# Sliding-window attention with a gated feed-forward on one core: one batch of products with v per unit, w2 measured by groups, and another prologue

## The chip, the core and the metric

The kernel runs on one core of a Trainium2 chip. The core has TensorE (PE; its weight loads are shown apart as PEld), VectorE (DVE), ScalarE (ACT), GpSimd (POOL) and SyncE (SP), which issues most DMAs. Each engine takes its instructions in a fixed order and waits on semaphores for the others. The metric is device time in microseconds (us) of one execution; lower is better.

## The reference

Input is one sequence of 2048 tokens with 512 channels. It is normalised per token; from the result come causal attention with a window of 256 (32 heads of 16 channels) and a gated feed-forward with 1792 hidden channels, and both are joined:

```python
def _A_ref(x, wqkv, wo):
    H = 32; Dh = D // H; W = 256
    q, k, v = ...(x @ wqkv)...
    scores = einsum("bhqd,bhkd->bhqk", q, k) * Dh ** -0.5
    mask = (idx[:, None] - idx[None, :] >= 0) & (idx[:, None] - idx[None, :] < W)
    p = softmax(where(mask, scores, -1e9))
    return (p @ v).reshape(B, S, D) @ wo

def _B_ref(x, w1, w3, w2):
    return (silu(x @ w1) * (x @ w3)) @ w2

xn = layernorm(x)
out = x + _A_ref(xn, A_wqkv, A_wo) * silu(_B_ref(xn, B_w1, B_w3, B_w2))
```

All is float32. The kernel makes most products from 16-bit halves: each operand is split into a high and a low float16 part, and three of the four partial products are summed. Before that every weight is scaled by a power of two that follows from the sums of squares of its columns.

## The kernel before

**Work.** The tokens are cut into four tiles of 512 (`t`), the heads into four groups of eight (`g`), and each group into two halves (`p`). One (`t`, `g`, `p`) is a unit; there are 32. A unit's attention has two passes. The first, `pass1`, makes scores with the queries on the rows of the array (L588), and VectorE takes their maxima (L600). The maxima go through a small transpose (L615), a copy `mt` (L621) and two DMAs into extra rows of `qa`, so that the second pass subtracts them inside its matmuls. `pass2` makes the scores again, with the keys on the rows (L662), in five chunks (four for the first tile); VectorE adds masks (L669), ScalarE takes the exponential into a buffer `pt` (L672), and `values` multiplies `pt` by v in float32 on array tiles of 64 x 32 (L690). `finish` then copies the sums out of the bank `po` into `os`: ScalarE one half (L700), VectorE adds the other (L703).

**Banks.** PSUM has two buffers `s` of two banks for scores, one buffer `po` of two banks, and two banks `m0`, `m1` for the dense products. `po` takes the products with v, and in between the scores of a few parts of the first pass.

**Order on TensorE.** TensorE's order is that of the code; the other engines' order comes from a scheduler. A plan, `PLAN` (`FIRST_PLAN` for the first tile), cuts a unit into five batches. In it W is one chunk of the second pass of this unit, M a part of the first pass of the unit after the next one, in a buffer `s`, X such a part in `po`; the numbers are the chunks whose products with v follow. Between the batches `spread` puts dense work: projections (L534), v (L504), w1 and w3 (`gate_up`, L836), w2 (`down`, L881), wo (`total`, L923). A batch with products counts 2.5 per chunk when the dense work is dealt out, a dense matmul counts 1. Small pieces can be queued some steps on (`later`), or to the next part of a first pass, whose bank then has room beside the scores (`beside_scores`, `maxima`, `besides`).

**Weights.** In the first tile of tokens, w1, w3 and w2 come from memory in 14 blocks `f` of 128 hidden channels, are measured, scaled and split, used, and stored in `dW1`, `dW2` for the other tiles. `load` fetches all three of a block; `measure` takes two blocks: six squares (`squares`, L231 on ScalarE, L233 on VectorE), their sums over partitions by matmuls with ones and the powers of two (`powers`, L258 or L263, L269 to L278), then the cuts of w1 and w3 (`split_pool`: L303 and L304 on ScalarE, L300 on GpSimd). `measure_down` finds one scale for each of the four groups of w2 and queues its cuts. All such tiles lie in 41 slots of 2 KB a partition, taken in turn.

**Prologue.** Token tiles 0 and 2 are fetched by SyncE's queue, 1 and 3 by ScalarE's. VectorE takes means and variances (L406, L407), a reciprocal root by a shifted integer and three Newton steps (`rstd`, L411 to L421), and centres the tokens (L424). TensorE transposes them (L440), ScalarE copies the high halves XH (L443). Meanwhile the weights of q and k of the first group are measured and cut (L290 to L295), and TensorE is kept busy with products of ones (`keep_busy`, L1108). The first projection (L534) needs all four XH and the cut weights.

## Time and profile before

| | us |
|---|---|
| median of 3 runs | 861.09 (858.77 to 861.37) |
| the profiled execution, time | 861.01 |
| its span in the profile | 859.2 |
| TensorE busy in the span | 820.9 |
| granted TensorE clock, mean | 0.992 |

The profile is of one execution. The page gives busy times, the chain of work that ended last, and groups of instructions by line; the trace behind it answers for timelines, waits and stretches of time. A matmul's end is modelled, since matmuls overlap, so distances between starts are the better measure. In a row of a timeline stand the start, the length from first start to last end, engine, line, operation, what is written and read, and in brackets the idle time before and what ended it.

### The profile page before, as it was taken

Reading aid. Unit: us, or ns where it says so; the run is one execution under the profiler, and the core shown is the slowest. Engines: PE = TensorE matmul, PEld = TensorE weight load, DVE = VectorE, ACT = ScalarE, POOL = GpSimd, SP = SyncE. Lnnn points to the kernel's source line nnn. Section 1 sums busy time; section 2 is a strip of 40 time slices with the busy share of each in tenths; the row PEclk is TensorE's granted clock in tenths of the full one; section 3 lists DMA queues with packets and bytes.
Section 4 is the critical chain, followed back from the end, with each engine's and each line's share of the span. In section 5 each row is a group of like instructions: output and inputs, shape, how many; then the busy total and the mean of one; then the engine's idle time right before and its main releaser. Section 6 shows DMA issues by size and latency. Waiting matters only on the chain.

```text
span 859.2 us, 22511 instructions
## 1 busy us (share of the span) xinstructions
PE 820.9 (96%) x8734; PEld 380.0 (44%) x8734; DVE 608.3 (71%) x2013; ACT 407.9 (47%) x598; POOL 198.0 (23%) x325
## 2 busy tenths in 40 slices
PE   9899888899999999998999999999999999999998
PEld 4344334444444444443444444444444444444444
DVE  8786656976787667797777876677676787675435
ACT  6898776273426444344343445443443444433521
POOL 2254256151113203111111112120211113031211
PEclk9999899999999999999999999999999999999999
DMA  9958446236643443452533432534442353333201
GB/s 303 292 195 258 144 143 183 74 101 193 174 121 89 116 118 110 147 151 64 132 104 86 144 104 80 164 118 106 143 128 89 102 153 84 112 102 90 62 13 59
DMA packets 95323, 110.62 MB, mean 129 GB/s; under 512 B 17200, under 2 KB 60528, under 8 KB 95216
## 3 DMA queue, kind: packets, MB, share of 16 engines
q1 hardware_dynamic: 94928, 108.67, 43.5%
q8 instruction: 68, 1.11, 0.6%
q10 hardware_dynamic: 288, 0.52, 0.2%
q14 instruction: 39, 0.32, 0.1%
HBM read 76.28 MB, written 28.57 MB: 122 GB/s over the span
## 4 chain that ended last, share of the span: by engine, by line
PE 57%; DVE 15%; issue 7%; DMA 7%; ACT 7%; POOL 4%; SPq 3%; DVEq 0%; POOLq 0%; ACTq 0%
PE m L836 20%; PE m L881 12%; PE po L690 6%; PE m L534 6%; DVE junk L600 5%; PE m L923 3%; POOL slot L300 3%; PE s L662 3%; PE m L504 3%; DVE s L669 2%; PE s L588 2%; ACT pt L672 1%; DMA slot<-in_A_x_dram 1%; DMA dr<-dd 1%; SPq L734 1%
## 5 line engine op out<-in xcount | busy, mean ns | idle before, releaser
L300 POOL TENSOR_TENSOR slot<-slot,slot 128x256 f16<-128x256 f32 (+1 forms) x228 | 149.5, 681 | 568.1 <-ACT slot L860 446.2
L836 PE MATMUL m<-XH,slot 128*128 128x512 f16 x896 | 267.5, 380 | 2.7 <-DVE slot L851 1.9
L672 ACT ACTIVATE pt<-s,es 128x1024 f32<-128x1024 f32 x152 | 167.8, 1113 | 198.9 <-DVE s L669 186.4
L836 PEld LDWEIGHTS <-slot 128*128 128x128 f16 x1344 | 125.1, 98 | 158.5 <-issue 16.3
L836 PE MATMUL m<-XL,slot 128*128 128x512 f16 x448 | 169.8, 379 | 0.0
L881 PE MATMUL m<-slot,slot 128*128 128x512 f16 x672 | 159.5, 387 | 3.1 <-DVE slot L851 1.9
L600 DVE CUSTOM_DVE_ANT_0 junk<-s,MW 128x320 bf16<-128x320 f32 x288 | 139.6, 485 | 30.8 <-PE s L588 20.1
L669 DVE TENSOR_TENSOR s<-s,MK 128x256 f32<-128x256 f32 (+2 forms) x280 | 118.8, 434 | 55.3 <-PE s L662 51.1
L881 PEld LDWEIGHTS <-slot 128*128 128x128 f16 x672 | 63.1, 99 | 84.0 <-issue 14.4
L690 PE MATMUL po<-pt,V 64*32 64x320 f32 (+4 forms) x2880 | 84.8, 345 | 1.3 <-ACT pt L672 1.1
L600 DVE CUSTOM_DVE_ANT_0 junk<-po,MW 128x320 bf16<-128x320 f32 x160 | 77.3, 483 | 6.7 <-DVE M L600 0.5
L860 ACT CAST slot<-slot 128x512 f16<-128x512 f32 x56 | 34.6, 618 | 74.9 <-DVE slot L856 72.8
L851 DVE SCALAR_TENSOR_TENSOR slot<-slot,m 128x512 f32<-128x512 f32 x56 | 38.4, 685 | 32.1 <-ACT slot L847 32.0
L690 PEld LDWEIGHTS po<-pt,V 64*32 64x32 f32 x2880 | 47.1, 106 | 30.8 <-issue 5.5
L662 PE MATMUL s<-qa,KA 50*64 50x320 f16 (+3 forms) x1472 | 58.0, 259 | 1.7 <-ACT pt L672 0.9
L847 ACT ACTIVATE slot<-m,sgs 128x512 f32<-128x512 f32 x56 | 38.3, 683 | 41.8 <-PE m L836 39.7
L662 PEld LDWEIGHTS <-KA 50*64 50x64 f16 x1472 | 32.6, 105 | 56.4 <-issue 36.1
L588 PE MATMUL s<-KA,qa 48*64 48x320 f16 (+2 forms) x648 | 46.5, 299 | 6.5 <-DVE M L600 3.6
L856 DVE SCALAR_TENSOR_TENSOR slot<-m,slot 128x512 f32<-128x512 f32 x56 | 38.4, 686 | 17.9 <-PE m L836 17.3
L897 DVE SCALAR_TENSOR_TENSOR slot<-m,dsc,slot 128x512 f32<-128x512 f32 x48 | 35.7, 745 | 20.0 <-PE m L881 19.9
L588 PEld LDWEIGHTS <-qa 48*64 48x64 f16 x1024 | 29.6, 106 | 39.8 <-issue 26.6
L534 PE MATMUL m<-XH,whi 128*128 128x512 f16 x120 | 45.5, 387 | 1.6 <-DVE slot L897 0.9
(151 smaller groups left out, 880.7 us busy)
## 6 DMA issues: line engine op xcount, KB each, us to landing
slot<-dW SPq DMA_DIRECT2D x126, 256.0 KB
slot<-in_B_w_dram SPq DMA_DIRECT2D x42, 256.0 KB
dW<-slot SPq DMA_DIRECT2D x42, 256.0 KB
slot<-in_A_x_dram SPq DMA_DIRECT2D x30, 256.0 KB
KA<-dK SPq DMA_DIRECT2D x24, 288.0 KB
qa<-dQ SPq DMA_DIRECT2D x32, 192.0 KB
dK<-slot SPq DMA_DIRECT2D x16, 256.0 KB
dQ<-slot SPq DMA_DIRECT2D x16, 256.0 KB
```

The source lines that it names most:

```text
L300: op(out[:, c], a[:, c], b[:, c])
L534: nc.tensor.matmul(cell["pp"], a[:, k, c, :], b[:, c, :], start=(c, i) == parts[0][0], stop=(c, i) == parts[-1][-1])
L588: nc.tensor.matmul(s[64 * c:64 * c + 64, r, :n], qa[rows, 2 * p + a, ii * P + 64 * c:ii * P + 64 * c + 64], ka[rows, 2 * p + a, e - n:e], ...
L600: nc.vector.tensor_tensor_reduce(out=junk[:, :n], in0=s[:, r, :n], in1=mask, scale=1.0, scalar=NEG, op0=ALU.add, op1=ALU.max, accum_out=M[ ...
L662: nc.tensor.matmul(s[64 * h:64 * h + 64, r, o:o + 64 * n], ka[rows, 2 * p + a, 64 * (m + 4):64 * (m + 5)], qa[rows, 2 * p + a, 64 * (m + k ...
L669: nc.vector.tensor_add(v, v, MK[:, kind, of:of + n, :].unsqueeze(1).to_broadcast([P, 2 * len(which), n, 64]))
L672: nc.scalar.activation(pt, s, AF.Exp, scale=es)
L690: nc.tensor.matmul(cell["po"][32 * i:32 * i + 32, h, 64 * (m + k):64 * (m + k + n)], V[64 * h:64 * h + 64, (4 * t + m // 2) % VB, hd * VW: ...
L836: nc.tensor.matmul(cell[k], w[:, (a * NC + c) * P:(a * NC + c + 1) * P], b[:, c, :], start=c == 0 and i == 0, stop=c == NC - 1 and i == 2)
L851: nc.vector.scalar_tensor_tensor(sg, sg, 1.0, cell[0], op0=ALU.add, op1=ALU.mult)
L856: nc.vector.scalar_tensor_tensor(sg, cell[1], 0.5 * HS / (WS * XS)**2, sg, op0=ALU.mult, op1=ALU.mult)
L881: nc.tensor.matmul(ps, hh[:, a * TW + b * P:a * TW + (b + 1) * P], w[:, c * D:(c + 1) * D], start=f == f0 and i == 0, stop=f == f1 - 1 and ...
```

## The change

It has four parts.

1. `values` is called once a unit, with all chunks, in the last batch. The X parts move from batches 1 to 3 into batches 2 to 4, the two chunks WW into batch 4. `pt` has five buffers (`ppool`), not four, and the slots go from 41 to 39.
2. w2 leaves `load` and `measure`. `load_down` fetches its blocks one by one, `measure_down` squares one block at a time on ScalarE, and at a group's last block takes the group's sums by `powers` beside scores, then the scale, then queues the cuts. `measure` has four squares.
3. The scale of a weight is no longer a reciprocal and a product but one integer operation on the power of two's bits. The root takes a step of higher order and one Newton step, with the constants folded in.
4. Token tile 0 is fetched in two halves by two queues, tile 1 by SyncE, 2 and 3 by ScalarE; the scale is ordered ahead of the centring; there are 25 and 3 fillers for 27 and 5.

```diff
-SLOTS = 41
+SLOTS = 39
...
-    ppool = pool("ppool", 4)
+    ppool = pool("ppool", 5)
...
# powers
+            if inv is not None:
+                lasts["scale"] = nc.vector.tensor_scalar(inv.bitcast(I32), al.bitcast(I32), -1.0,
+                                                         (2 * 127 - 63 + WS_EXP) * 2.0**23, op0=ALU.mult, op1=ALU.add)
             nc.vector.tensor_scalar(p2, al, 2.0**63, None, op0=ALU.mult)
-            nc.vector.reciprocal(inv, p2)
...
# prepare: load, rstd
+            if t == b == 0:
+                for h in range(2):
+                    r = slice(64 * h, 64 * h + 64)
+                    (nc.scalar if h else nc.sync).dma_start(xts[b][r], x[r, :])
+                return
+            (nc.scalar if t == 0 and b > 1 else nc.sync).dma_start(xts[b], x[t * TW + b * P:t * TW + (b + 1) * P, :])
...
-            for i in range(3):
+            nc.vector.tensor_mul(sq, r0, r0)
+            nc.vector.tensor_mul(sq, sq, ve)
+            nc.vector.scalar_tensor_tensor(sq, sq, -10 / 3, sq, op0=ALU.add, op1=ALU.mult)
+            nc.vector.scalar_tensor_tensor(r0, sq, 5.0, r0, op0=ALU.add, op1=ALU.mult)
+            with nullcontext() if t else tc.issue_after(lasts["cast"].ins):
                 nc.vector.tensor_mul(sq, r0, r0)
-                nc.vector.scalar_tensor_tensor(sq, sq, -0.5, ve, op0=ALU.mult, op1=ALU.mult)
-                nc.vector.scalar_tensor_tensor(r0, sq, 1.5, r0, op0=ALU.add, op1=ALU.mult)
-            nc.vector.tensor_scalar(rs[:, b0:b1], r0, XS, None, op0=ALU.mult)
+            nc.vector.scalar_tensor_tensor(sq, sq, -0.5 * (3 / 8)**3 * XS, ve, op0=ALU.mult, op1=ALU.mult)
+            nc.vector.scalar_tensor_tensor(rs[:, b0:b1], sq, 1.5 * (3 / 8) * XS, r0, op0=ALU.add, op1=ALU.mult)
...
# load, measure, measure_down
-        nc.sync.dma_start(raw2, w2[f * P:(f + 1) * P, :])
...
-        sb = squares([raws[0][0], raws[1][0], raws[0][1], raws[1][1], RAW[f][1], RAW[f + 1][1]], on_act=6 if f > 2 else 4, apart=apart)
+        sb = squares([raws[0][0], raws[1][0], raws[0][1], raws[1][1]], on_act=4 if f > 2 else 2, apart=apart)
...
+    def load_down(f):
+        RAW2[f] = raw = take(F32)
+        nc.sync.dma_start(raw, w2[f * P:(f + 1) * P, :])
+
+    def measure_down(k, f):
+        f0, f1 = GROUPS[k]
+        n = f1 - f0
...
+        nc.scalar.activation(sq, RAW2[f], AF.Square, accum_out=NORMS[k][:, f - f0:f - f0 + 1])
+        if f < f1 - 1:
+            return
+        sb = small.tile([P, n], BF16, name="sb2")
+        nc.vector.tensor_copy(sb, NORMS[k])
+        def scale(s):
+            p2 = small.tile([P, n], F32, name="pp2")
+            return then(s, powers(sb, n, p2, None, s), lambda: rest(p2))
...
+        beside_scores(2, scale)
...
# plans
-    FIRST_PLAN = (("WMX", ()), ("WMX", ()), ("WMX", ()), ("WM", (0, 1)), ("M", (2, 3)))
-    PLAN = (("WMX", ()), ("WMX", ()), ("WWX", ()), ("WM", (0, 1, 2)), ("MM", (3, 4)))
+    FIRST_PLAN = (("WM", ()), ("WMX", ()), ("WMX", ()), ("WMX", ()), ("M", (0, 1, 2, 3)))
+    PLAN = (("WM", ()), ("WMX", ()), ("WMX", ()), ("WWX", ()), ("MM", (0, 1, 2, 3, 4)))
...
# prologue
-    keep_busy(27)
+    keep_busy(25)
...
-    keep_busy(5)
+    keep_busy(3)
     rstd0(0, 4)
-    for b in range(4):
-        centre0(b)
-    with tc.issue_after(lasts["centre"].ins):
-        qk[0][3]((1,))
+    with tc.issue_after(lasts["scale"].ins):
+        for b in range(4):
+            centre0(b)
+    qk[0][3]((1,))
```

On TensorE, in a unit of a later tile of tokens, the two groups of products with v stood apart before, the first ahead of a product for v (L504), the second, after 12 dense matmuls and eight score matmuls, ahead of one with wo (L923). Rows of equal matmuls are put together with their count; `po`, `pt` and `V` are the sums, the exponentials and v.

```order
L690 MATMUL po<-pt,V 32x256 x8
L690 MATMUL po<-pt,V 32x320 x8
L690 MATMUL po<-pt,V 32x192 x8
L504 LDWEIGHTS XH
L504 MATMUL m_5900<-wvh,XH 128x512
```

```order
L690 MATMUL po<-pt,V 32x320 x8
L690 MATMUL po<-pt,V 32x128 x4
L690 MATMUL po<-pt,V 32x64 x8
L690 MATMUL po<-pt,V 32x128 x4
L923 LDWEIGHTS slot_2418
L923 MATMUL m_5976<-slot_4177,slot_2418 128x512
```

The changed program, same unit, has one group (its line is now 698), behind the eight score matmuls of the last batch.

```order
L698 MATMUL po<-pt,V 32x256 x8
L698 MATMUL po<-pt,V 32x320 x8
L698 MATMUL po<-pt,V 32x192 x8
L698 MATMUL po<-pt,V 32x320 x8
L698 MATMUL po<-pt,V 32x128 x4
L698 MATMUL po<-pt,V 32x64 x8
L698 MATMUL po<-pt,V 32x128 x4
L950 LDWEIGHTS slot_3945
```

The matmuls are the same; the first 24 moved behind the dense work and the scores that stood between. Six dense matmuls follow the group now, where 12 followed each of the two, and between WWX and the last batch stand 18.

On VectorE, at the change from one unit to the next, the addition into `os` was followed before, within the first batch, by the maxima of an X in the other use of `po` (`junk<-po`) and by the copy `mt` from it.

```order
L703 TENSOR_TENSOR os_6333<-os_6333,po_6226 128x512
L669 TENSOR_TENSOR s_6361<-s_6361,MK_119 128x4x2x64
L851 SCALAR_TENSOR_TENSOR slot21_6357<-slot21_6357,m0_6344 128x512
L600 ISA junk_6378,M_6360<-s_6373,MW_111 128x320
L600 ISA M_6360 128x1
L600 ISA junk_6380,M_6360<-s_6373,MW_111 128x320
L600 ISA M_6360 128x1
L600 ISA junk_6389,M_6360<-po_6382,MW_111 128x320
L600 ISA M_6360 128x1
L600 ISA junk_6391,M_6360<-po_6382,MW_111 128x320
L600 ISA M_6360 128x1
L621 CAST mt_6393<-po_6382 32x128
```

In the changed program (lines 711, 677, 878, 608 and 883 do what 703, 669, 851, 600 and 856 did) the next rows from `po` come a batch later.

```order
L711 TENSOR_TENSOR os_6354<-os_6354,po_6305 128x512
L677 TENSOR_TENSOR s_6375<-s_6375,MK_119 128x4x2x64
L878 SCALAR_TENSOR_TENSOR slot9_6371<-slot9_6371,m0_6278 128x512
L608 ISA junk_6392,M_6374<-s_6387,MW_111 128x320
L608 ISA M_6374 128x1
L608 ISA junk_6394,M_6374<-s_6387,MW_111 128x320
L608 ISA M_6374 128x1
L883 SCALAR_TENSOR_TENSOR slot9_6371<-m1_6397,slot9_6371 128x512
L677 TENSOR_TENSOR s_6423<-s_6423,MK_119 128x4x64
```

The X, its maxima and `mt` moved behind the next dense products; 24 dense matmuls stand on TensorE between the last product with v and the next X, where 12 stood, with few exceptions.

In the prologue, VectorE before: the end of the root, the four centrings (L424), and between them the steps of the scale `sw` of the first weights.

```order
L421 TENSOR_SCALAR rs<-r_303 128x4
L424 TENSOR_SCALAR slot_163<-slot_163,mv,rs 128x512
L269 TENSOR_SCALAR al<-s 128x1
L424 TENSOR_SCALAR slot_165<-slot_165,mv,rs 128x512
L275 TENSOR_SCALAR al<-al 128x1
L424 TENSOR_SCALAR slot_167<-slot_167,mv,rs 128x512
L277 TENSOR_SCALAR p2qk_283<-al 128x1
L424 TENSOR_SCALAR slot_169<-slot_169,mv,rs 128x512
L278 RECIPROCAL invqk_284<-p2qk_283 128x1
L384 TENSOR_SCALAR es_355<-p2qk_283 128x1
L290 TENSOR_SCALAR sw_293<-invqk_284 128x1
```

The same place in the changed program:

```order
L270 TENSOR_SCALAR al<-s 128x1
L429 SCALAR_TENSOR_TENSOR rs<-sq,r_289 128x4
L276 TENSOR_SCALAR al<-al 128x1
L280 TENSOR_SCALAR sw_274<-al 128x1
L282 TENSOR_SCALAR p2qk_273<-al 128x1
L432 TENSOR_SCALAR slot_162<-slot_162,mv,rs 128x512
L432 TENSOR_SCALAR slot_165<-slot_165,mv,rs 128x512
L432 TENSOR_SCALAR slot_167<-slot_167,mv,rs 128x512
L432 TENSOR_SCALAR slot_169<-slot_169,mv,rs 128x512
```

The scale is done ahead of the centring. On ScalarE the first cut of the weights (`whi`) accordingly moved from between the second and third copy of XH to ahead of the first.

More of the change, by code (lines that the diff above doesn't have):

```diff
@@ L40 @@
 XS = 2.0**10
-WS = 2.0**13
+WS_EXP = 13
+WS = 2.0**WS_EXP
 QS = 2.0**5
@@ L242, in cast @@
         def cast():
-            nc.vector.tensor_copy(sb, ssq)
+            lasts["cast"] = nc.vector.tensor_copy(sb, ssq)
         if apart:
@@ L324, in scale @@
             p2 = const.tile([P, 1], F32, name=f"p2{name}")
-            inv = const.tile([P, 1], F32, name=f"inv{name}")
-            def rest():
-                cell["p2"], cell["inv"], cell["sw"] = p2, inv, scaled(inv, WS, f"sw{name}")
-            return then(s, powers(cell["sb"], 1, p2, inv, s), rest)
+            cell["p2"], cell["sw"] = p2, const.tile([P, 1], F32, name=f"sw{name}")
+            return then(s, powers(cell["sb"], 1, p2, cell["sw"], s))
         def cut(apart=0):
@@ L364, in scale @@
             p2 = const.tile([P, 1], F32, name=f"p2qk{g}")
-            inv = const.tile([P, 1], F32, name=f"invqk{g}")
-            def rest():
-                cell["p2"], cell["sw"] = p2, scaled(inv, WS, f"sw{g}")
-            return then(s, powers(cell["sb"], 1, p2, inv, s), rest)
+            cell["p2"], cell["sw"] = p2, const.tile([P, 1], F32, name=f"sw{g}")
+            return then(s, powers(cell["sb"], 1, p2, cell["sw"], s))
         def cut(ks=(1, 0)):
@@ L761, in load @@
             return
-        RAW[f] = raw, raw2 = [take(F32) for _ in range(2)], take(F32)
+        RAW[f] = raw = [take(F32) for _ in range(2)]
         for k, w in enumerate((w1, w3)):
@@ L765, in load @@
                               w[:, f * P:(f + 1) * P].rearrange("(c p) f -> p c f", p=P))
[L766 removed]
     measured = set()
     def measure(f, apart=0):
[L772 to L773 removed]
+        raws = [RAW.pop(f + i) for i in range(2)]
+        sb = squares([raws[0][0], raws[1][0], raws[0][1], raws[1][1]], on_act=4 if f > 2 else 2, apart=apart)
         def scale(s=None):
[L776 to L778 removed]
+            pp = small.tile([P, 2, 2], F32, name="pp")
+            pi = small.tile([P, 2, 2], F32, name="pi")
+            return then(s, powers(sb, 4, pp.rearrange("p a b -> p (a b)"), pi.rearrange("p a b -> p (a b)"), s),
                         lambda: rest(pp, pi))
@@ L965, in feed_forward @@
                 if t == 0:
-                    if f % 2 or f == 0:
-                        pieces += [(0, lambda f=f: load(0, f)) for f in (range(f + LEAD, min(f + LEAD + 2, FB)) if f else range(4, LEAD + 1))]
+                    if (f % 2 or f == 0) and f + LEAD < FB - 2:
+                        pieces += [(0, lambda f=f: load(0, f)) for f in (range(f + LEAD, f + LEAD + 2) if f else range(4, LEAD + 1))]
+                    elif f + LEAD == FB - 1:
+                        pieces += [(0, lambda f=f: load(0, f)) for f in range(FB - 2, FB)]
                     if f % 2 and f + 3 < FB:
                         pieces.append((0, lambda f=f + 3: measure(f, 1)))
-                    pieces += [(0, lambda k=k: measure_down(k)) for k, (_, f1) in enumerate(GROUPS) if f == f1 - 1]
+                    pieces += [(0, lambda f=f: load_down(f)) for f in range(f + 2 if f else 0, min(f + 3, FB))]
+                    for m in range(f + 1 if f else 0, min(f + 2, FB)):
+                        k = next(k for k, (_, f1) in enumerate(GROUPS) if m < f1)
+                        pieces.append((0, lambda k=k, m=m: later(2, lambda: measure_down(k, m))))
                 else:
```

54 lines of the change are left out of this document (26 added, 28 removed).

## The prediction, made before the changed kernel was run

> **What bounds the kernel now.** I began with the page: busy shares and the chain of work that ended last.
>
> ```profile
> PE 820.9 (96%) x8734; PEld 380.0 (44%) x8734; DVE 608.3 (71%) x2013; ACT 407.9 (47%) x598; POOL 198.0 (23%) x325
> PE 57%; DVE 15%; issue 7%; DMA 7%; ACT 7%; POOL 4%; SPq 3%; DVEq 0%; POOLq 0%; ACTq 0%
> ```
>
> TensorE is busy in 820.9 of the 859.2 us, so a change can win in two ways only: less TensorE work, or part of the 38.3 us in which it idles. No other engine is near its end; where they stand in the chain, they make TensorE wait. Next I asked for busy time by stage (columns: length, then busy time and instructions of PE, PEld, DVE, ACT and POOL, then the granted clock).
>
> ```profile
> 30.00:210.00 180.00, 160.16 (x1571) 72.61 (x1570) 131.08 (x529) 124.92 (x234) 75.58 (x116) 0.97 0.55 168
> 420.00:640.00 220.00, 217.01 (x2546) 101.81 (x2545) 159.49 (x507) 92.86 (x114) 37.25 (x56) 1.00 0.41 117
> ```
>
> From 30 to 210 us, where the first 512 tokens run and the weights are measured and cut, TensorE idles 19.8 us, half of all its idle time. From 420 to 640 us it idles 3.0 us. The view of waits says who ends the idle time (total us, times, longest).
>
> ```profile
> PE po L588 <- DVE os L703: 9.0, 8, 3.8
> PE s L588 <- DVE M L600: 3.6, 2, 2.9
> PE s L588 <- ACT pt L672: 2.1, 5, 0.7
> PE s L258 <- DVE al L273: 2.0, 1, 2.0
> ```
>
> The largest is one that the change touches: a first-pass score matmul (L588) that writes the bank `po` waits until `finish` of the unit before has copied its sums out of `po` (L700 on ScalarE, then L703 on VectorE).
>
> **One unit before.** The TensorE timeline of one unit of the third 512 tokens shows its five small batches; between them stand 12 or 18 dense 128x512 matmuls.
>
> ```profile
> 547.47 0.42 PE L662 MATMUL s<-qa,KA 50*64 50x320 f16 x12
> 547.72 0.31 PE L588 MATMUL s<-KA,qa 48*64 48x320 f16 x4
> 547.96 1.53 PE L690 MATMUL po<-pt,V 64*32 64x256 f32 x48
> 549.42 0.60 PE L836 MATMUL m<-XH,slot 128*128 128x512 f16 x2
> ...
> 552.11 0.47 PE L588 MATMUL s<-KA,qa 48*64 48x320 f16 x8
> 552.51 1.26 PE L690 MATMUL po<-pt,V 64*32 64x320 f32 x48
> 553.70 2.76 PE L923 MATMUL m<-slot,slot 128*128 128x512 f16 x12
> 556.39 0.41 PE L662 MATMUL s<-qa,KA 50*64 50x256 f16 x8
> 556.63 0.31 PE L588 MATMUL s<-KA,qa 48*64 48x320 f16 x4
> 556.77 0.30 PE L588 MATMUL po<-KA,qa 48*64 48x320 f16 x4
> ...
> 557.03 0.39 PE L534 MATMUL m<-XH,whi 128*128 128x512 f16 x1
> ...
> 561.02 0.41 PE L662 MATMUL s<-qa,KA 50*64 50x320 f16 x8
> ...
> 561.64 0.61 PE L836 MATMUL m<-XH,slot 128*128 128x512 f16 x2
> ...
> 565.63 0.64 PE L662 MATMUL s<-qa,KA 50*64 50x320 f16 x20
> 566.09 0.31 PE L588 MATMUL po<-KA,qa 48*64 48x320 f16 x4
> 566.34 0.60 PE L836 MATMUL m<-XH,slot 128*128 128x512 f16 x2
> ```
>
> From the start of a batch to the next dense matmul: the batch with the first products with v (547.47 to 549.42) 1.95 us, the one with the second (552.11 to 553.70) 1.59, then 0.64, 0.62 and, with two second-pass chunks, 0.71: together 5.51 us.
>
> **A. The products with v in one batch.** The same matmuls are issued, in a new grouping. A batch of W and M alone takes 0.24 (556.39 to 556.63) and about 0.24 more until a dense matmul (566.09 to 566.34 is such a step): 0.48. Two batches WMX take 0.64 and 0.62 as now. WWX has 24 second-pass matmuls for 20; 12 took 0.25 (547.47 to 547.72) and 20 took 0.46, so 0.71 becomes 0.76. The last batch takes 1.59 plus the other group's 1.46 (547.96 to 549.42), less what is saved at the joint, where no switch of the array lies between the groups. The trace has no such joint. It saves at least nothing and at most one entrance, which is 0.24 (547.72 to 547.96); between ends so far apart no row is nearer, and I take the middle, 0.12, so 2.93. The sum is 0.48 + 0.64 + 0.62 + 0.76 + 2.93 = 5.43, which saves 0.08 a unit: **A = -2.6 us** over 32 units, with ends at +1.3 and -6.4.
>
> [...] The rows show an entrance and an exit, not which part of them a joint keeps.
>
> **B. The wait for `os`.** The first X of a unit moves from the first batch to the second. Before, 12 dense matmuls (2.69 us, 553.70 to 556.39) stand between the last product with v and this X; the order after has 24 almost everywhere, plus one batch, so X comes about 2.7 + 0.5 = 3.2 us later after the work it waits for. The longest wait:
>
> ```profile
> 148.79 0.62 ACT L304 CAST slot<-slot 128x512 f16<-128x512 f32 x1 [2.65 <-POOL slot L300]
> ...
> 149.94 0.56 ACT L700 COPY os<-po 128x512 f32<-128x512 f32 x1
> 150.54 0.62 DVE L703 TENSOR_TENSOR os<-os,po 128x448 f32<-128x448 f32 x1 [4.88 <-ACT os L700]
> ...
> 151.21 0.25 PE L588 MATMUL po<-KA,qa 48*64 48x128 f16 x4 [3.85 <-DVE os L703]
> ```
>
> ScalarE stood still for a slot that GpSimd was still reading, and the copy queued behind it. Of 3.85 us, 0.7 are left; the other seven waits, 5.2 us in all, vanish: **B = -8.3**, between 0 (all of it returns elsewhere) and -9.0.
>
> **C. The waits for exponentials.**
>
> ```profile
> 567.11 2.19 ACT L672 ACTIVATE pt<-s,es 128x1024 f32<-128x1024 f32 x2 [0.69 <-DVE s L669]
> ```
>
> The two exponentials of the batch at 565.63 end at 569.30, 3.67 us after it, while after 12 dense matmuls the next batch comes about 3.40 us on; its M needs the second one's bank, hence 2.1 us in 5 waits. After the change 18 dense matmuls follow WWX (4.7 us), so these waits go. In exchange only 12 stand before WWX in about half the units; its X then needs the maxima of the X before. With five `pt` buffers the fifth exponential no longer waits for the first products with v. I take **C = -1.0**, between -2.1 and +2.
>
> **D. The granted clock.**
>
> ```profile
> 151.40:155.60 4.20, 4.20 (x18) 1.62 (x13) 4.17 (x15) 1.10 (x1) 0.00 (x0) 0.59 0.15 38
> 390.50:395.00 4.50, 4.50 (x15) 1.71 (x15) 2.95 (x11) 1.19 (x2) 1.40 (x2) 0.62 0.29 93
> ```
>
> Behind the 3.85 us wait the clock was 0.59 for 4.2 us, a loss of 4.2 x 0.41 = 1.7. Without the wait this should go; the loss at 390 us (4.5 x 0.38 = 1.7) I leave. **D = -1.7**, between 0 and -3.4.
>
> **E. The prologue.** First the page's row of the token tiles (issues, KB each), then the timeline.
>
> ```profile
> slot<-in_A_x_dram SPq DMA_DIRECT2D x30, 256.0 KB
> ```
>
> ```profile
> 4.39 1.29 DVE L406 BATCH_NORM_STATS2 st<-slot 128x6 f32<-128x512 f32 x2 [1.27 <-DMA slot<-in_A_x_dram]
> ...
> 7.33 0.17 DVE L411 TENSOR_SCALAR ve<-mv 128x4 f32<-128x4 f32 x1
> ...
> 9.92 0.55 DVE L424 TENSOR_SCALAR slot<-slot,mv,rs 128x512 f32<-128x512 f32 x1
> ...
> 12.07 0.66 PE L440 MATMUL s<-identf,slot 128*128 128x128 f32 x4
> 12.13 0.15 DVE L290 TENSOR_SCALAR sw<-invqk 128x1 f32<-128x1 f32 x1
> ...
> 12.31 0.72 ACT L294 ACTIVATE whi<-slot,sw 128x512 f16<-128x512 f32 x1
> ...
> 13.41 0.59 ACT L443 CAST XH<-s 128x512 f16<-128x512 f32 x1
> 14.05 1.02 PE L534 MATMUL s<-XH,whi 128*128 128x512 f16 x4
> ```
>
> From 7.33 to 9.92 stand 13 small steps of the root, 0.20 us each, and a cast. After, the root takes 10, but the scale (al, shift, sw, p2) comes ahead of the centring: 14 steps, so centring starts about 0.25 later and the last transposes end near 13.0 instead of 12.73. They are no longer followed by a wait: the 0.72 us of `whi` lay between the casts of XH and now lies ahead of them. The last cast ends near 13.6, not 14.00: -0.4. The first tokens may also land earlier; the two statistics at 4.39 start back to back, so 256 KB were not there much before 512 KB. At 0.65 a statistic this is worth 0 to 0.65; I take 0.4. **E = -0.8**, between 0 and -1.3. [...]
>
> [...]
>
> **F. w2 by groups.** The 14 loads of 256 KB and 14 squares are moved, not removed; four groups now have their own 4 power matmuls beside scores. Four such small matmuls take 0.14 (556.63 to 556.77): **F = +0.6**. VectorE loses 14 steps and gains about 24 of 0.15 us, hidden in its 49 idle us of that stage; uncovered they would cost 1.5. Two slots fewer could hold SyncE, behind whose waiting load all later loads and stores queue; but w2's raw tiles now arrive one by one instead of with w1 and w3, so fewer are held. No wait of TensorE above names such a load: 0, with 2 us as the upper end.
>
> **The sum.** B, C and D give -11.0. A TensorE that comes earlier meets other late results, such as the 3.6 us for `M`, so I give back a quarter, +2.7. In all -2.6 - 11.0 + 2.7 - 0.8 + 0.6 = -11.1. The profiled execution took 861.01 us (the median of the runs is 861.09, 1.8 over the span): 849.9, rounded to **850.0 us**.
>
> **Rivals.** *The waits return in full.* VectorE and ScalarE have their work to do in 30 to 210 us, and the chain runs through them for 22%. Then only A, E and F count: 861.0 - 2.8 = 858.2. Against it: VectorE is free for 49 us there and GpSimd for 104, and the wait shown above came from the order of a queue, not from a full engine. Chance 0.15. *The joint saves nothing*, because the streams of fp32 set the groups' length: A is +1.3 and the time 853.9. For it: the group of small pieces takes 1.19 with 8 column blocks against 1.46 with 12, which is much overhead inside the group. Chance 0.10. *Slower:* every unit now ends WWX, 18 dense matmuls, MM, and both banks of MM wait for the two exponentials. There is room: they may end 4.8 us after WWX, and end at 3.67. If two more ScalarE instructions (0.6 each) and one dense product came ahead, they would end at 5.7 and TensorE would wait 0.9 in each of 24 units, 21.6 us: about 871.6. It decides from 1.1 us of delay on; at 0.5 us of waiting a unit the gain is used up. ScalarE is busy 93 of 220 us there, which speaks against it. Chance 0.05.
>
> **How the numbers follow.** The forecast has 0.70, its own range 842 to 855: the good ends of A to E all at once would give 839, which I leave out. The range for 8 in 10 is 842 to 858, which takes in the second rival and half of the first. About 0.3%, 2.6 us, is what a measurement can tell from no change. Faster is the forecast, the second rival and about half of the first, 0.87; within 0.3% is the rest of the first, 0.08; slower is the third, 0.05.
>
> **What would show it.** A: one group of products with v per unit, shorter than 2.65 us. B: no wait of `po` for `os` over 1 us. C: fewer waits for `pt`. D: full clock near 150 us. E: the first projection near 13.3 us. The prediction falls if TensorE's idle time stays near 38 us, or if waits for `pt` or `M` appear in every unit.

## The result, and the profile after

The changed kernel takes **836.76 us** (median of 4 runs, 835.88 to 837.63); the kernel before took 860.56 beside it (858.77 to 861.37). The ratio is 0.9726, with a 95% interval of 0.9707 to 0.9746: 23.8 us faster, where 11 were forecast. The direction was right; the time lies 5 us below the low end of the range.

The page of the changed kernel, busy shares and the chain that ended last:

```profile
span 835.8 us, 22561 instructions
PE 809.2 (97%) x8746; PEld 382.2 (46%) x8746; DVE 609.5 (73%) x2005; ACT 408.8 (49%) x598; POOL 196.9 (24%) x325
PE 68%; issue 9%; DVE 8%; DMA 4%; POOL 3%; ACT 3%; SPq 3%; POOLq 0%; ACTq 0%; DVEq 0%
```

TensorE's busy time fell from 820.9 to 809.2 us and its idle time from 38.3 to 26.6: each gave 11.7. The chain now runs through VectorE and ScalarE for 11%, not 22%. By stage:

```profile
30.00:210.00 180.00, 164.10 (x1633) 76.25 (x1632) 132.32 (x537) 126.46 (x233) 70.61 (x110) 0.99 0.60 182
420.00:640.00 220.00, 219.90 (x2620) 104.77 (x2604) 166.04 (x526) 93.33 (x114) 34.61 (x52) 1.00 0.41 116
```

Idle time fell from 19.8 to 15.9 us between 30 and 210 us, and from 3.0 to 0.1 between 420 and 640. The waits of TensorE:

```profile
PE s L596 <- DVE M L608: 3.6, 2, 2.8
PE s L259 <- DVE al L274: 2.9, 1, 2.9
PE po L596 <- DVE XL L480: 2.4, 3, 1.1
PE s L596 <- ACT pt L680: 1.9, 3, 0.7
...
PE s L259 <- DVE sq L427: 1.4, 1, 1.4
PE s L670 <- ACT pt L680: 1.1, 2, 0.6
```

No wait for `os` is left. One unit of the third 512 tokens on TensorE, the matching stage to the rows of before:

```profile
509.16 0.47 PE L596 MATMUL s<-KA,qa 48*64 48x320 f16 x8
509.56 2.55 PE L698 MATMUL po<-pt,V 64*32 64x256 f32 x96
512.04 1.47 PE L908 MATMUL m<-slot,slot 128*128 128x512 f16 x6
513.44 0.41 PE L670 MATMUL s<-qa,KA 50*64 50x256 f16 x8
513.68 0.31 PE L596 MATMUL s<-KA,qa 48*64 48x320 f16 x4
513.92 2.76 PE L908 MATMUL m<-slot,slot 128*128 128x512 f16 x12
...
517.91 0.41 PE L670 MATMUL s<-qa,KA 50*64 50x320 f16 x8
...
518.56 0.39 PE L542 MATMUL m<-XH,whi 128*128 128x512 f16 x1
...
522.54 0.41 PE L670 MATMUL s<-qa,KA 50*64 50x320 f16 x8
...
523.16 0.61 PE L863 MATMUL m<-XH,slot 128*128 128x512 f16 x2
...
528.45 0.64 PE L670 MATMUL s<-qa,KA 50*64 50x320 f16 x24
528.91 0.31 PE L596 MATMUL po<-KA,qa 48*64 48x320 f16 x4
529.16 0.61 PE L863 MATMUL m<-XH,slot 128*128 128x512 f16 x2
```

From the start of a batch to the next dense matmul: 2.88 (509.16 to 512.04), 0.48, 0.65, 0.62 and 0.71, together 5.34 us for 5.51 before.

**Stretches at half clock.** In both profiles the granted clock falls to 0.50 for 3.41 us, or twice that. Windows laid on these stretches (the granted clock is the third number from the end) show, before:

```profile
94.07:100.89 6.82, 6.20 (x24) 2.36 (x25) 2.58 (x14) 4.49 (x10) 0.04 (x1) 0.50 0.40 139
152.09:155.50 3.41, 3.41 (x10) 1.21 (x9) 3.41 (x13) 1.00 (x1) 0.00 (x0) 0.50 0.18 44
391.03:394.44 3.41, 3.41 (x10) 1.21 (x8) 2.42 (x10) 1.11 (x1) 1.21 (x2) 0.50 0.26 75
```

and after:

```profile
12.37:15.78 3.41, 3.41 (x16) 2.53 (x15) 2.31 (x5) 2.80 (x5) 0.00 (x0) 0.50 0.91 242
94.29:97.70 3.41, 3.41 (x12) 1.32 (x13) 2.11 (x12) 3.38 (x8) 0.00 (x0) 0.50 0.25 84
```

Before, dense matmuls start 0.22 us apart up to the stretch at 391.03 (390.44, 390.66, 390.88) and 0.43 within it (391.15, 391.58, 392.00), so I count half of each stretch, 1.7 us, as lost by a busy TensorE. Every run lists its mean granted clock, so for each kernel the **clock loss**, (1 - mean clock) x span, can be averaged over its runs. It is 7.2 us before (52 runs of the kernel before, taken beside the others) and 3.8 after. One further run of the kernel before, 935.89 us at a clock of 0.848, is left out. The clock has three digits, so this is good to some 0.4 us. The table below parts each time into this loss and the rest, which is the mean time less the loss.

### The profile page after: what moved, and what is told of

Same layout as the page of the kernel before. It is cut to its first block, busy times and chain, and to the rows that moved or that the text cites. A ratio compares the mean times of both kernels' runs of the same rounds, so it can differ in the third digit from the quotient of the medians.

```text
span 835.8 us, 22561 instructions
## 1 busy us (share of the span) xinstructions
PE 809.2 (97%) x8746; PEld 382.2 (46%) x8746; DVE 609.5 (73%) x2005; ACT 408.8 (49%) x598; POOL 196.9 (24%) x325
## 4 chain that ended last, share of the span: by engine, by line
PE 68%; issue 9%; DVE 8%; DMA 4%; POOL 3%; ACT 3%; SPq 3%; POOLq 0%; ACTq 0%; DVEq 0%
PE m L863 25%; PE m L908 13%; PE po L698 8%; PE m L542 6%; PE s L670 5%; PE m L950 4%; POOL slot L304 3%; PE m L512 3%; DVE junk L608 2%; PE s L596 2%; DMA slot<-in_B_w_dram 2%; DVE s L677 1%; PE po L596 1%; SPq L742 1%; ACT slot L307 1%
## 5 line engine op out<-in xcount | busy, mean ns | idle before, releaser
L608 DVE CUSTOM_DVE_ANT_0 junk<-s,MW 128x320 bf16<-128x320 f32 x276 | 134.3, 487 | 24.9 <-PE s L596 15.7
L608 DVE CUSTOM_DVE_ANT_0 junk<-po,MW 128x320 bf16<-128x320 f32 x172 | 83.7, 487 | 5.6 <-DVE al L276 0.4
L698 PE MATMUL po<-pt,V 64*32 64x320 f32 (+4 forms) x2880 | 77.7, 344 | 0.1
L698 PEld LDWEIGHTS po<-pt,V 64*32 64x32 f32 x2880 | 52.0, 106 | 23.6 <-PE s L596 5.0
L878 DVE SCALAR_TENSOR_TENSOR slot<-slot,m 128x512 f32<-128x512 f32 x56 | 38.3, 684 | 29.7 <-ACT slot L874 28.0
L670 PEld LDWEIGHTS <-KA 50*64 50x64 f16 x1472 | 30.3, 106 | 56.2 <-issue 35.4
L874 ACT ACTIVATE slot<-m,sgs 128x512 f32<-128x512 f32 x56 | 38.3, 684 | 27.4 <-PE m L863 26.8
L542 PE MATMUL m<-XL,whi 128*128 128x512 f16 x120 | 44.5, 379 | 0.0
```

Of the source, the lines that this page charges most:

```text
L542: nc.tensor.matmul(cell["pp"], a[:, k, c, :], b[:, c, :], start=(c, i) == parts[0][0], stop=(c, i) == parts[-1][-1])
L608: nc.vector.tensor_tensor_reduce(out=junk[:, :n], in0=s[:, r, :n], in1=mask, scale=1.0, scalar=NEG, op0=ALU.add, op1=ALU.max, accum_out=M[ ...
L670: nc.tensor.matmul(s[64 * h:64 * h + 64, r, o:o + 64 * n], ka[rows, 2 * p + a, 64 * (m + 4):64 * (m + 5)], qa[rows, 2 * p + a, 64 * (m + k ...
L698: nc.tensor.matmul(cell["po"][32 * i:32 * i + 32, h, 64 * (m + k):64 * (m + k + n)], V[64 * h:64 * h + 64, (4 * t + m // 2) % VB, hd * VW: ...
L874: nc.scalar.activation(sg, cell[0], AF.Tanh, scale=sg_scale[:, f:f + 1])
```

## The experiments

My first theory was that the plans give nearly all of the gain, by the waits for `os` and by a joint that saves a switch of the array; its rival, that much comes from the parts that I had priced at nothing. Later theories are named where they are tested. The table is a staircase from the kernel before to the changed one, one part at a time; each row is a kernel of its own.

| kernel | what it adds to the row above | median us | ratio to before, 95% | clock loss | rest |
|---|---|---|---|---|---|
| before | | 860.56 | | 7.2 | 852.5 |
| b_s39 | 39 slots | 853.40 | 0.9923 (0.9904 to 0.9941) | 7.0 | 845.8 |
| b_plan39 | new plans, five `pt` | 843.22 | 0.9815 (0.9788 to 0.9842) | 5.9 | 837.2 |
| b_w2plan39 | w2 by groups | 838.28 | 0.975 (0.9731 to 0.9769) | 1.9 | 836.4 |
| pro_old | new root and scale | 833.56 | 0.9706 (0.9686 to 0.9727) | 1.2 | 832.5 |
| loads_old | scale ahead of centring, fewer fillers | 833.51 | 0.9694 (0.9676 to 0.9713) | 2.7 | 830.9 |
| the change | token loads in halves, two queues | 836.76 | 0.9726 (0.9707 to 0.9746) | 3.8 | 833.0 |

The rows were measured on different chips, on which the kernel before took 859.0 to 860.6 us; each ratio is to the runs on the same chip. Differences between rows of about 1 us are therefore not to be read.

### Undoing parts of the change

**X back in batches 1 to 3, products with v still in one batch.**

```diff
-    FIRST_PLAN = (("WM", ()), ("WMX", ()), ("WMX", ()), ("WMX", ()), ("M", (0, 1, 2, 3)))
-    PLAN = (("WM", ()), ("WMX", ()), ("WMX", ()), ("WWX", ()), ("MM", (0, 1, 2, 3, 4)))
+    FIRST_PLAN = (("WMX", ()), ("WMX", ()), ("WMX", ()), ("WM", ()), ("M", (0, 1, 2, 3)))
+    PLAN = (("WMX", ()), ("WMX", ()), ("WWX", ()), ("WM", ()), ("MM", (0, 1, 2, 3, 4)))
```

> The changed kernel with the X parts back in the first three batches; the products with v stay in one batch, everything else as changed. Theory 1 (the place of X carries the larger part of the gain, because it ends the waits of po for os): about 9 to 12 us more than the changed kernel, 846 to 849 us, and waits of po for os of 6 us or more in all. Theory 2 (the joint of the products carries it): at most 3 us more, 837 to 840 us.

852.80 us, 16 more than the changed kernel (ratio to before 0.9915, 0.9889 to 0.9941). Its largest wait:

```profile
PE po L596 <- DVE os L711: 13.3, 10, 4.1
```

The wait is back, and longer than before (9.0), which fits the order: six dense matmuls and not twelve stand between the products and the X. The place of X is what removed it. The time lies above the range of either theory. The clock loss is 11.9 us: 8 of the 16 us are slower clock, 7.6 the rest.

**Products with v in two batches, X placed as in the change; and, differently, the last two chunks' products behind the six dense matmuls, with no batch more.** In the first, `FIRST_PLAN` is split in the same way.

```diff
-    PLAN = (..., ("MM", (0, 1, 2, 3, 4)))
+    PLAN = (..., ("MM", (0, 1, 2)), ("", (3, 4)))
```

```diff
-                if cs:
+                if len(cs) > 3:
+                    cols(*cs[:-2])
+                    rest_of.append(lambda: cols(*cs[-2:]))
+                elif cs:
                     cols(*cs)
...
+        if dense and rest_of:
+            run(dense)
+            dense = []
+        while rest_of:
+            rest_of.pop(0)()
```

> The changed kernel with the products with v in two groups again, the second in a batch of its own with dense work between; X as changed. From the traces one group takes 2.88 us with its MM, two would take 1.86 and 1.19 and one more entrance from dense work of 0.09: 0.26 us a unit. Theory 1 (the array drains at each switch): 6 to 9 us more than the changed kernel, 843 to 846 us. Theory 2 (the streams alone set the time): 0 to 2 us more, 837 to 839 us.

> The changed kernel with the last two chunks' products with v behind the six dense matmuls that follow the group, ahead of the next unit's first scores; no batch is added and nothing else moves. One more change between dense work and products a unit. Theory 1 (the array drains at each switch; the trace has 0.16 us less at the joint and some 0.1 for the other entrance): 5 to 9 us more than the changed kernel, 842 to 846 us. Theory 2 (streams set the time; the loss of the version with a sixth batch, 22.7 us, was waits alone): 836 to 839 us.

The first took 859.49 us (0.9996, 0.9984 to 1.0008), more than either theory had. It says nothing on the joint alone: a sixth batch deals the dense work in six parts, so less of it covers the exponentials, which now end late:

```profile
PE s L596 <- ACT pt L680: 9.7, 13, 2.2
PE s L670 <- ACT pt L680: 3.3, 3, 2.0
```

The second avoids that, has no wait for `os`, and took 843.07 us (0.9803, 0.978 to 0.9826), 6.3 above the change, 5.7 of it in the rest. The rows of the products, from the pages of the kernel before, the change and this one, show the price of a joint:

```profile
L690 PE MATMUL po<-pt,V 64*32 64x320 f32 (+4 forms) x2880 | 84.8, 345 | 1.3 <-ACT pt L672 1.1
```

```profile
L698 PE MATMUL po<-pt,V 64*32 64x320 f32 (+4 forms) x2880 | 77.7, 344 | 0.1
```

```profile
L698 PE MATMUL po<-pt,V 64*32 64x320 f32 (+4 forms) x2880 | 84.1, 345 | 0.0
```

The same 2880 matmuls keep the array 6.4 to 7.1 us longer when they come in 64 groups, not 32: 0.20 to 0.22 us for each group saved. The other profiles bear this out: the row has 77.7 us in all ten kernels with one group a unit, and 84.1 in seven of the nine with two (84.8 and 87.0 in the others; 83.7 in v_apart, which has two in all but the last units).

**The old plans, all else as changed.** `FIRST_PLAN` and the plans of the last units are the old ones too.

```diff
-    PLAN = (("WM", ()), ("WMX", ()), ("WMX", ()), ("WWX", ()), ("MM", (0, 1, 2, 3, 4)))
+    PLAN = (("WMX", ()), ("WMX", ()), ("WWX", ()), ("WM", (0, 1, 2)), ("MM", (3, 4)))
```

> The changed kernel with the old plans (X in the first batches and products in two batches); five pt buffers, 39 slots, w2 by groups and the new prologue stay. Theory 1 (the plans carry nearly the whole gain): 20 to 24 us more than the changed kernel, 857 to 861 us. Theory 2 (w2 by groups or the fifth pt buffer carries a part of its own): 845 to 853 us.

849.85 us (0.9884, 0.9863 to 0.9904), with 8.2 us of waits for `os` in nine. The plans are worth 13 us in the finished kernel (10.5 without the clock), about half of the gain; the other half lies elsewhere, which my forecast did not have.

### Slots

**The kernel before with fewer slots, and with the fifth `pt` buffer.**

```diff
-SLOTS = 41
+SLOTS = 39
...
-    ppool = pool("ppool", 4)
+    ppool = pool("ppool", 5)
```

> The kernel before with a fifth pt buffer and 39 slots, nothing else. With old plans the changed kernel still took 849.9 us, 10.4 less than the kernel before though its loads in the prologue cost 3.3; some 13.7 us come from elsewhere. Theory 1 (the fifth pt buffer: the exponential of the fifth chunk no longer holds ScalarE until the first products with v have read the first buffer): 848 to 853 us. Theory 2 (w2 by groups): 858 to 862 us, or slower by the missing slots.

> The kernel before with 39 slots for 41, nothing else. Theory S: 4 to 9 us more than the kernel before, 863 to 868 us. Theory R: 858 to 861.5 us.

> The kernel before with 40 slots for 41, nothing else. With 39 it took 853.4 us, 6 less than with 41. Theory C (the number only decides by chance which tile follows which in a slot, and so which waits occur): 40 gives something unordered between 850 and 862, and where the wait of ScalarE for a slot that GpSimd reads is there ahead of 151 us, the time is 858 or more, where it is not, 856 or less. Theory L (fewer slots make the loads later and so better placed): 40 lies between, 855 to 858.

> The kernel before with 38 slots. Theory C (chance of the assignment): anywhere between 850 and 862, not in order with 41, 40 and 39. Theory L (fewer is better): 848 to 852.

With both edits 853.98 us (0.9938, 0.9917 to 0.9958), with 39 slots alone 853.40, which no theory had: the fifth buffer is worth nothing by itself. 40 slots gave 852.67 (0.9923, 0.9899 to 0.9946), 38 gave 855.32 (0.9955, 0.9939 to 0.9971). So there is no order by number; 41 is the odd one. Of ScalarE's casts behind GpSimd, the largest before was the one at 148.79 us that the prediction shows (2.65 us); with 39 slots these are all:

```profile
123.20 0.62 ACT L304 CAST slot<-slot 128x512 f16<-128x512 f32 x1 [0.52 <-POOL slot L300]
...
126.97 0.62 ACT L304 CAST slot<-slot 128x512 f16<-128x512 f32 x1 [1.00 <-POOL slot L300]
```

The waits for `os` fall with it, from 9.0 to 4.1 us in all. Slots are taken in turn, so their number decides which tile must wait for which earlier reader. But that one wait is not where the 6 to 7 us come from. With 39 slots other waits stand in its place:

```profile
PE s L588 <- DVE M L600: 4.6, 2, 3.8
PE po L588 <- DVE os L703: 4.1, 5, 1.2
PE s L588 <- DVE XL L472: 4.0, 2, 3.2
```

Before, the wait of score matmuls in `s` for `M` was 3.6 us and that for XL (L472) 0.3. The addition into `os` of the eighth unit ends at 270.0 us before and at 269.8 with 39 slots, so up to there nothing is won (a further stretch at half clock, 1.7 us, counts in this); 5.0 us are won in the next eight units and 2.1 in the last sixteen. A long wait of ScalarE for GpSimd does not mark the slow kernel either, since 40 slots have a longer one:

```profile
ACT slot L917 <- POOL slot L300: 14.8, 5, 7.0
```

And w2 by groups with 41 slots (b_w2, below), as slow as the kernel before, waits 8.8 us for `os`, 3.3 at most, with no such cast ahead: there the copy stood behind a square of a weight that had waited 2.5 us for a DMA, and cuts. What these runs show is that, of the kernels with the old plans and the old root, the two with 41 slots have a wait for `os` of over 3 us and the five with 38 to 40 none over 1.3, and that 41 slots cost 5 to 8 us. Which waits make that up stays open.

### w2, root and scale

**w2 by groups alone; with five `pt` and 39 slots; with the new plans too (b_w2plan39); and b_plan39, which has the plans without w2.** The edit is the w2 part of the diff (`load_down`, `measure_down`), the plans are those of the change.

> The kernel before with w2 fetched, measured and cut by groups, nothing else (four pt buffers, 41 slots, old plans, old prologue). Theory 2 (w2 by groups carries some 10 us, in the first tile of tokens): 848 to 853 us, and TensorE idles 6 us or more less between 30 and 210 us. Theory 1 (the fifth pt buffer does): 859 to 862 us.

> The kernel before with w2 by groups, five pt buffers and 39 slots; old plans, old root, scale and prologue. Theory S (39 slots cost time when w2's raw tiles come with w1 and w3, and the grouping gives that back): 845 to 849 us, against 854.0 with the fifth buffer and 39 slots alone. Theory R (the shorter root and the scale from the bits are what came on top): 852 to 855 us.

> The kernel before with the new plans, five pt buffers and 39 slots; w2 and the prologue as before. If the parts add up and the fifth buffer is the second part: 834 to 838 us. If w2 by groups is: 845 to 849 us.

> The kernel before with the new plans, five pt buffers, 39 slots and w2 by groups; its loads, prologue, root and scale stay as before. With the new plans but without w2 by groups it took 843.2 us, with both and the new root and scale 833.6. Theory W (w2 by groups, worth nothing by itself, is worth about 9 us once the new plans have taken the other waits away): 833 to 837, and the waits for M, al and the exponentials in 30 to 210 us, 9.1 us in the kernel without it, fall to about 2. Theory R (the new root and scale, which shorten the powers of two and so the step from a weight's squares to its cuts, give it): 841 to 844.

Alone it is worth nothing that can be measured: 858.47 us (0.9996, 0.998 to 1.0013). On b_pt39 it gives 4 us (850.05; 0.9897, 0.9869 to 0.9925), on b_plan39 5 us (838.28 for 843.22). None of the four times lies in a range that was forecast (b_w2 misses one by 0.5 us). Without the clock loss the gains are 0, 1.2 and 0.8, no more than the chips differ by: the moved squares free almost no time, but fewer stretches run at half clock (the loss falls by 0.9, 2.2 and 4.0 us). Of the waits that Theory W named, the one for `al` and the long one for the exponentials are gone, the 2.9 us for `M` stay.

**The change with old loads, order and fillers; only the new root and scale stay.**

```diff
...
-    keep_busy(25)
+    keep_busy(27)
...
-    keep_busy(3)
+    keep_busy(5)
     rstd0(0, 4)
-    with tc.issue_after(lasts["scale"].ins):
-        for b in range(4):
-            centre0(b)
-    qk[0][3]((1,))
+    for b in range(4):
+        centre0(b)
+    with tc.issue_after(lasts["centre"].ins):
+        qk[0][3]((1,))
```

> The changed kernel with the old loads of the token tiles, the old order of scale, centring and first cut, and the old fillers; the shorter root and the scale from the bits stay. With the old loads alone it took 833.5 us. If the new order saves what the prediction said (0.4 us or a little more): 833.7 to 834.5 us. If the order does nothing or harm: 832.5 to 833.5 us.

833.56 us, so the new order, with 833.51, is worth nothing that can be measured. Against b_w2plan39, which differs in the root and scale alone, this is 4.7 us less by the medians and 3.8 by the ratios, most of it outside the clock. It is not the prologue: the first projection starts at 14.02 there and at 14.09 here. In the profiles this kernel pulls ahead by 3.9 us in the first 240 us, where every weight's powers of two stand between its squares and its cuts (and by 1.9 more at a stretch of half clock between 210 and 420 us that it lacks: granted clock 0.99 there, 1.00 here); which wait it shortens I did not isolate.

### The prologue

**The token loads of before, all else as changed; and tile 0 in halves with the other tiles on their old queues.** The first edit is this one; the second changes its last line only.

```diff
-            if t == b == 0:
-                for h in range(2):
-                    r = slice(64 * h, 64 * h + 64)
-                    (nc.scalar if h else nc.sync).dma_start(xts[b][r], x[r, :])
-                return
-            (nc.scalar if t == 0 and b > 1 else nc.sync).dma_start(...)
+            (nc.scalar if t == 0 and b % 2 else nc.sync).dma_start(...)
```

> The changed kernel with the token tiles of the prologue fetched as before (tiles 0 and 2 by SyncE, 1 and 3 by ScalarE, whole). Theory 1 (the new issue order makes the tiles land later: the last statistics began at 7.6 us against 6.5): the first projection begins 1 to 1.5 us earlier than the 15.98 of the changed kernel, 835 to 836 us. Theory 2 (the landing times were chance): no difference in the landing beyond 0.3 us, 836 to 838 us.

> The changed kernel with tile 0 in two halves but tiles 1 and 3 by ScalarE and tile 2 by SyncE, as before. The old loads gave 833.5 us. If the halves are what lands late (issuing a half took 0.57 us, a whole tile 0.42): 836 to 837.5 us, the last statistics at 7 us or later. If the assignment of whole tiles to queues is: 833 to 834.5 us.

With the old loads 833.51 us, **with pro_old the best of all kernels here**, 3.3 under the change (2.8 by the ratios). With halves and the old queues 837.72 (0.9742, 0.9718 to 0.9765): the halves are the cause. The issues and statistics, with old loads:

```profile
0.73 0.90 ACTq L400 DMA_DIRECT2D slot<-in_A_x_dram  x2
0.74 0.87 SPq L400 DMA_DIRECT2D slot<-in_A_x_dram  x2
...
4.45 1.29 DVE L404 BATCH_NORM_STATS2 st<-slot 128x6 f32<-128x512 f32 x2 [1.33 <-DMA slot<-in_A_x_dram]
...
5.87 1.27 DVE L404 BATCH_NORM_STATS2 st<-slot 128x6 f32<-128x512 f32 x2
```

and in the changed kernel, with what follows:

```profile
0.74 0.59 SPq L403 DMA_DIRECT2D slot<-in_A_x_dram  x1
0.74 0.56 ACTq L403 DMA_DIRECT2D slot<-in_A_x_dram  x1
...
1.33 1.08 ACTq L405 DMA_DIRECT2D slot<-in_A_x_dram  x2
...
1.39 0.81 SPq L405 DMA_DIRECT2D slot<-in_A_x_dram  x1
...
4.39 0.69 DVE L409 BATCH_NORM_STATS2 st<-slot 128x6 f32<-128x512 f32 x1 [1.27 <-DMA slot<-in_A_x_dram]
...
7.58 0.69 DVE L409 BATCH_NORM_STATS2 st<-slot 128x6 f32<-128x512 f32 x1 [0.48 <-DMA slot<-in_A_x_dram]
...
15.98 1.03 PE L542 MATMUL s<-XH,whi 128*128 128x512 f16 x4
```

Half a tile took 0.56 to 0.59 us to issue, a whole one with old loads 0.45 (0.90 for two). In these two profiles the first tile is hardly there earlier (4.39 for 4.45), and the last statistic starts at 7.58, where with old loads the last two start at 5.87 and are done by 7.14. The root waits for it, and the first projection comes at 15.98; before it came at 14.05. The other profiles agree: in the seven kernels with halves the first statistic starts at 3.94 to 4.39 us, the last at 7.58 to 9.15 and the first projection at 15.43 to 16.67; in the thirteen with whole tiles at 4.36 to 4.50, 6.38 to 6.60 and 13.85 to 14.23. So the halves of the first tile land some 0.25 us earlier in the mean, and the later tiles over 1 us later. The last token load is issued by 2.41 us, not by 1.63; this could account for 0.8 us of the delay, the rest is not explained.

### The clock

**Fillers in a wait: nine products of ones ahead of the first-pass scores that waited for `M` near 90 us, in the kernel with old loads; and six for three in the changed kernel's prologue.** They compute nothing that is used.

```diff
                 for k, f in enumerate(rows):
+                    if fill and k == 1:
+                        keep_busy(9)
                     f()
```

```diff
-    keep_busy(3)
+    keep_busy(6)
     rstd0(0, 4)
```

> The changed kernel with the token loads of before (833.5 us), and nine products of ones in the second unit's first batch, between the second-pass scores and the first-pass scores that waited 2.2 us for the maxima near 90 us; they fill TensorE's idle time and compute nothing that is used. In 16 profiles every stretch of 3.41 us in which TensorE idled 2.0 us or more was followed by one at half clock. Theory K (the idle time causes it, and a wait so costs half of 3.41 us more than its length): no half clock between 85 and 100 us, the wait under 0.5 us, later units 1.7 us earlier, 831.8 us. Rival (something else at this time lowers the clock, the weight traffic say): half clock for 3.4 us near 90 us as before, 833.5 us.

> The changed kernel (836.8 us) with six products of ones for three ahead of the transposes in the prologue; nothing else. Its profile has half clock from 12.37 to 15.78 us, after a stretch with 1.9 us idle. Theory K: with about 0.65 us less idle time there no half clock before 30 us, the four products of ones after the transposes take 1.0 us and not 1.7, the first projection starts at 15.3 us and not 15.98, and the time is 835.5 to 836.5. Rival (the late statistics alone set it): half clock and 15.98 as before, 836.8.

The first: 836.97 us (0.9738, 0.9723 to 0.9754), not the 831.8 expected. TensorE, with the fillers (L1140):

```profile
87.92 2.12 PE L1140 MATMUL m<-onesb 128*128 128x512 bf16 x9
90.15 0.25 PE L591 MATMUL s<-KA,qa 48*64 48x128 f16 x4
93.55 2.75 PE L903 MATMUL m<-slot,slot 128*128 128x512 f16 x12 [3.15 <-ACT slot L916]
```

The wait for `M` is gone, but the fillers took a bank of `m` out of turn, and the next dense product waited 3.15 us for ScalarE to empty the other. So the time says nothing on the price. The clock does: the half clock that stood near 90 us, behind a wait of 2.16 us for `M`, is gone (window 85 to 100, clock 0.89 with old loads, 1.00 here).

```profile
85.00:100.00 15.00, 12.84 (x123) 5.61 (x108) 10.10 (x38) 11.40 (x26) 3.04 (x5) 0.89 0.56 182
```

```profile
85.00:100.00 15.00, 11.74 (x132) 5.53 (x116) 9.14 (x33) 10.47 (x26) 3.38 (x6) 1.00 0.55 178
```

The second: 838.30 us (0.9758, 0.9741 to 0.9776). The idle time lay ahead of the place that I filled (2.41 us until the sums of squares at 10.56), and half clock came at 11.02 (0.50 from 11.02 to 14.44), the first projection at 16.27 and not 15.3: a miss.

**The kernel with old loads and 38 slots** (`SLOTS = 38`).

> The changed kernel with the token loads of before, and 38 slots for 39; with 39 it took 833.5 us. Theory C (chance of the assignment, in this kernel too): off by more than 2 us, either way, with a wait of several us that the other does not have. Its rival: with the new plans nothing of a unit waits on the slots' order any more, since 24 dense matmuls stand where 12 stood: 832 to 835.

834.54 us (0.9704, 0.9681 to 0.9727), within a microsecond of 39. With the new plans the number of slots no longer matters, at least between these two.

## Why the prediction was wrong in size

The mechanism was right: products in one batch, X later, no wait for `os`, fewer half clocks. What failed is the pricing of the parts beside the plans. By the table, the new plans (with the fifth `pt`, worth nothing alone) gave -10.2 us on the kernel with 39 slots (and -13 in the finished kernel), where A to D with the give-back forecast -10.9. All else, forecast at -0.2, gave -13.6: slots -7.2, w2 by groups -4.9, root and scale -4.7, loads +3.3. These steps depend on the order in which the parts are added; w2 by groups alone is worth nothing. That the plans' sum fits is partly luck: A was over twice as large, and with 39 slots only 4.0 us of B's waits were left to remove. By its own steps:

- **A**, forecast -2.6: by the unit's rows (5.51 - 5.34) x 32 = -5.4, by the kernel with the products behind the dense work -5.7, by the products' rows -6.4: more than twice the forecast, at the far end of its range. The last batch takes 2.88 us where the prediction set 2.93, so the joint saves 0.17 and not 0.12, and WWX costs 0.71 and not 0.76. I had no row for a joint and took the middle of 0 and 0.24. The products' rows (0.20 to 0.22 a group) come close to the whole 0.24. What the array does at such a change, which theories of v_apart and v_behind name, no profile shows; the rows show its price alone.
- **B**, forecast -8.3: the 9.0 us of waits for `os` are gone in full. Right for the waits, at the far end.
- **The give-back, +2.7** ("A TensorE that comes earlier meets other late results, such as the 3.6 us for `M`, so I give back a quarter"). In the whole nothing came back: TensorE's idle time fell by 11.7 us, 2.7 more than the waits for `os`, though the prologue had got worse, and the wait for `M` is still 3.6 us. But the whole holds other parts that shorten waits, so this does not refute the step. Single parts show what it meant: with 39 slots the waits for `os` fell by 4.9 us and those in `s` for `M` and XL rose by 4.7, and where the plans then removed the last 4.0 us, one of 3.1 us for an exponential came up (b_plan39, L662).
- **C**, forecast -1.0: waits for `pt` were 4.1 us in all (2.1, 1.1 and 0.9) and are 3.0 (1.9 and 1.1), so -1.1. The size fits, the place does not: of the 2.1 us that were to go, 1.9 are still there.
- **D**, forecast -1.7: four stretches at half clock became two, and the loss over all runs went from 7.2 to 3.8 us, -3.4. I counted one stretch, behind the longest wait. The one near 391 us follows three waits of some 0.7 us each, and went too.
- **E**, forecast -0.8: wrong sign. The loads alone cost 3.3 us. The order of scale and centring saved 0.2 us up to the first projection (13.85 with old loads, 14.05 before), not 0.4. For an earlier landing I took 0.4, and the first tile landed some 0.25 us earlier in the mean. But issue time was not saved (0.56 to 0.59 us for a half, 0.45 for a whole tile), and the later tiles came over 1 us late.
- **F and the slots**, forecast +0.6: w2 by groups is worth nothing by itself; with the new plans it gave 5 us, most of it by the clock, which the step had no term for. **The slots are the step that failed by most** ("No wait of TensorE above names such a load: 0, with 2 us as the upper end"): I looked only for loads that come later, and the runs show 5 to 7 us less with 38 to 40 slots in the kernel before, each against the runs on its own chip. There the waits for `os` that B names fall from 9.0 to 4.1 us, so B and the slots remove in part the same waits and don't add up. Which waits make the slots' gain stays open, and no run has the new plans with 41 slots.
- **Not priced:** the shorter scale outside the prologue. I priced its steps only up to the first projection; with the root it gives some 4 us (pro_old against b_w2plan39).

Against the profile: -11.7 of idle time, -5.4 to -6.4 for A and -3.4 for D make -20.5 to -21.5 of the 23.4 us by which the span fell. The remaining 2 to 3 I can't place.

**The rivals.** That the waits return in full (858.2 us) fell with the idle time, that the joint saves nothing (853.9) with the products' rows. The slower one, exponentials late for MM, did not come: 0.1 us idle in 220. The mechanism exists, though: with a sixth batch the waits for `pt` came to 13.0 us, and the time was that of before.

## What to carry to other kernels

Price every part of a change, also those that move no work: here the part that was priced step by step came out near its size, and the parts put at nothing gave about half of the gain. Look above all for edits that change who waits for whom without seeming to (a buffer count, an order of tiles), and ask of a wait that goes which other one may take its place. Where the profile has half clock behind a wait of TensorE, as behind the one of 3.85 us here, add its loss (1.7 us here) to the wait. Price a shortened step everywhere it is used, and a split transfer by its issue time as well (here 0.56 to 0.59 us for a half, 0.45 for the whole).

## What the runs showed of the hardware

**Half clock stood behind stretches in which TensorE idled long.** The stretches at half clock start whole multiples of 3.41 us apart: 58.02 us (17 times 3.413) and 238.94 (70 times) before, 81.92 (24 times) after, 54.61 (16 times) in x_back (40.77 to 95.38) and in b_s39 (95.40 to 150.01). Counted from the start of the span, this grid begins at 1.91 us before, at 2.13 after and at 0.78 in fill_pro, so its place differed from run to run. I laid it over the 20 profiles of this study, some 4900 stretches that lie whole in their spans, and compared each stretch's clock with TensorE's idle time in the one before. After 2.0 us idle or more the clock was half in 36 cases of 36; after 1.4 to 2.0 us in 15 of 63; after less in 4 of 4806, and these four follow a stretch at half clock. In the profiles of before and after, half clock followed 2.86 us idle (90.65 to 94.07, before), 2.53 (148.68 to 152.09, before), 2.81 (90.88 to 94.29, after), 1.80 (387.61 to 391.03, before) and 1.86 (8.96 to 12.37, after); full clock followed 1.85 (77.00 to 80.41, before) and 1.66 (39.68 to 43.09, after). The fillers near 90 us removed a wait of 2.16 us, and the half clock with it (0.89 to 1.00 from 85 to 100 us). The filler run fits: its 3.15 us of waiting fell across two stretches, 1.48 and 1.78 us, and no half clock followed, whereas of three waits of 0.71 to 0.77 us near 391 us before 1.80 us fell into one stretch, and half clock followed. So in these profiles it was not a wait's length that went with the half clock, but how much idle time fell into one stretch. Of the kernel with old loads, single runs lost 1.7 to 4.2 us to the clock.

**A DMA of half as many partitions was not cheaper to issue here**: 0.56 to 0.59 us for 64 rows of 2 KB in the seven kernels with halves, 0.39 to 0.47 for 128 rows in the thirteen without. The whole tiles issued behind the halves took 0.45 to 0.83.
